# One add on 128 channels for a batch's logits, filling products ahead of the last slot products, and new places for every step of the plan

## The chip, the cores and the metric

The kernel runs on one core of a Trainium2 chip. The metric is the device time of one execution in microseconds (us). The engines go by the profile's names: PE is TensorE (PEld its weight loads), DVE VectorE, ACT ScalarE, POOL GpSimd, SP the engine whose queue issues most DMAs.

## The reference

Attention within hash buckets over 4 batches of 8 heads, 768 positions of 64 numbers each, then a soft mixture of 8 experts with 4 slots each over the 3072 x 512 result.

```python
q_bits = (np.einsum('bhsd,dk->bhsk', q, proj) > 0)      # six bits, a bucket number
mask = q_bucket[:, :, :, None] == k_bucket[:, :, None, :]
scores = np.where(mask, scale * (q @ k.T), -1e9)
attn = softmax(scores); x = attn @ v                     # per head
...
logits = x @ phi                                         # 3072 x 32
d = exp(logits - logits.max(0)); d /= d.sum(0) + 1e-09
slot_input = d.T @ x                                     # per expert: 4 slots of 512
h = maximum(slot_input[e] @ w1[e], 0); slot_out[e] = h @ w2[e]
c = exp(logits - logits.max(1)); c /= c.sum(1) + 1e-09
return c @ slot_out
```

## The kernel before, in words

All 32 heads run through one software pipeline, two heads (a pair) at a time. For a pair, `load` (482) brings q and k in two DMAs into the buffers raw0 and raw1, which have one copy each; `bits` (635) projects them; `split_hi` (581) casts both to a high half on ACT (592) and `split_lo` (594) takes the rest: for x = 0 on DVE (from head 4 on), for x = 1 on POOL, both at line 596 and both from two SBUF inputs. `spread_*` and `move` (598) bring these into the operands X and Y, by DMA on SP's queue. `first_x`, `first_y` and the like do the same for the first heads.

For a head h, `smax` (683) makes 12 products with the bits, into PSUM tiles of a pool with two buffers; `most` (697) takes row maxima of them on DVE and so gives the buffers back; `shift` and `shift_rows` (724, 737) turn the maxima into a row that one more DMA (mr) writes into X and Y. `scores(h, i, part)` (747) makes the scores with that row, into PSUM tiles of a pool with three buffers, `exps(h, n)` (758) exponentiates a tile on ACT and gives its buffer back. `acc(h, n)`, n = 1 to 5 (764), adds up exponentials on POOL, 128 x 768 at a time; the last head's n > 2 run on DVE. `av(h, i)` (774) multiplies with v. `acc(h, 2)` needs exponentials that `exps(h, 4)` and `exps(h, 6)` make, `acc(h, 4)` those of 8 and 10, `acc(h, 5)` those of 10 and 11.

For a pair, `pair_sum`, `pair_turn`, `pair_rec` (789 to 811) make the reciprocals of the row sums, `pair_log` and `pair_add` (813, 822) the share of the pair in its batch's logits, `pair_x` (839) the outputs. After four pairs the batch is done: `batch_both` (885) adds the two halves of the logits, `batch_max` (896) is a chain of small DVE instructions, `batch_exp`, `batch_turn`, `batch_slots` (949, 48 products into the slots, 957), `batch_weigh`, `batch_share`, `batch_arrange` do the rest. The last batch does this in a tail of its own (`one_*`, `batch_fold`, `batch_slots`), then the experts' two layers run (1190 on) on weights that `load_weights` (466) brings piece by piece.

The order is written out by hand: `at` (1043) gives every step a due place, from the table FIRST for the first heads, LAST for the last ones, else WHEN (its lists have one entry for even and one for odd heads), in units of a sixth of a head, and the plan is sorted by it (1128). Each engine and SP's queue take their instructions in the order of the sorted plan, and wait there for what they need.

Of the kernel before, what the change touches and what calls it, by code (L numbers as in the profile page):

```python
# [9 lines left out]
F32 = mybir.dt.float32  # L10
F32R = mybir.dt.float32r
AF = mybir.ActivationFunctionType
ALU = mybir.AluOpType
# [32 lines left out]
WHEN = {'load': -18.5437,  # L46
 'bits': -14.5981,
 'bits_over': -14.5078,
 'split_hi': -9.9694,
 'split_lo': [-9.8385, -9.8378],  # L50
 'spread': [[-9.8341, -9.7926, -8.3674, -3.7564], [-9.232, -8.9609, -8.9193, -8.8534]],
 'load_v': [-2.0731, 0.304],
 'smax': [[-6.5818, -6.2731, -4.3769, -3.4458, -4.5967, -3.7676, -3.5906, -3.9389, -2.661, -2.8254, -2.6599, -3.084], [-8.0753, -7.9227, -7.3452, -6.8708, -5.9483, -2.1659, -2.1447, -5.982, -2.2765, -1.3212, -1.255, -1.427]],
 'scores': [[4.5824, 6.3832, 6.4644, 4.2001, 3.9067, 7.1017, 7.7467, 5.1054, 8.1238, 5.4296, 7.4038, 5.2071], [2.8436, 2.465, 2.9648, 2.4657, 5.7327, 3.0748, 3.2444, 3.2884, 4.4451, 6.0219, 6.0296, 4.6638]],
 'shift': [-2.4326, -0.5749],
 'shift_rows': [-2.1527, 0.4391],
 'acc': [[8.5792, 9.0133, 10.0698, 10.5707, 12.1884], [4.5656, 6.6965, 8.4071, 9.7438, 9.7613]],
 'av': [[7.8325, 8.0552, 9.4787, 9.5207, 9.724, 9.7353], [6.5159, 6.7171, 8.6714, 9.1161, 9.1578, 9.6194]],
 'pair_sum': 21.4738,
 'pair_turn': 21.5156,  # L60
 'pair_rec': 21.5212,
 'pair_log': 21.5499,
 'pair_x': [25.7118, 30.2518],
 'pair_add': 22.5706,
 'batch_both': 24.1116,
 'batch_max': 26.5961,
 'batch_exp': 31.1234,
 'batch_turn': 32.6363,
 'batch_scale': 58.0306,
 'batch_slots': 33.1739,  # L70
 'batch_weigh': 32.9664,
 'batch_share': 33.3424,
 'batch_arrange': 33.3585,
 'load_weights': 29.1076,
 'most': [[-5.7734, -3.5266, -3.0352, -3.6373, -3.1083, -3.355, -2.5228, -2.4882, -2.8978], [-6.6907, -6.2627, -5.1645, -3.8385, -1.1223, -4.3733, -2.2387, -0.7783, -0.8368]],
 'exps': [[5.4955, 6.513, 5.4191, 5.1659, 8.0415, 5.6129, 8.4248, 8.0422, 5.629], [3.1683, 3.4874, 2.9413, 6.3976, 3.6406, 5.4799, 6.1309, 6.353, 8.0514]]}

FIRST = {('bits', 0): -102.0988,
 ('first_x', 0): -24.247,
 ('first_x', 1): -39.392,  # L80
 ('first_x', 2): -29.078,
 ('first_x', 3): -19.8151,
 ('load', 4, 0): -5.2093,
 ('load', 4, 1): -3.4609,
 ('bits', 2): -21.6367,
 ('split_hi', 2): -5.8363,
 ('split_lo', 2, 0): 0.2624,
 ('split_lo', 2, 1): -4.3782,
 ('spread_y', 2): -4.8648,
 ('spread_bits', 2): -12.8087,  # L90
 ('spread_l', 2): 6.144,
 ('spread_x', 2): 3.6219,
 ('smax', 1, 0, 0): -22.4884,
 ('smax', 1, 0, 1): -14.425,
 ('smax', 1, 1, 0): -13.675,
 ('smax', 1, 1, 1): -18.5454,
 ('smax', 1, 2, 0): -15.9696,
 ('smax', 1, 2, 1): -10.3836,
 ('smax', 1, 3, 0): -10.2744,
 ('smax', 1, 3, 1): -13.2403,  # L100
# [1242 lines left out]
```

## Time and profile before

| | |
|---|---|
| runs shown | 481.4, 485.52, 1116.75 us; median 485.52 us |
| the profiled execution | 484.55 us |
| its span, first to last instruction | 482.8 us |
| PE busy | 452.3 us, 94% |
| DVE, ACT, POOL busy | 361.5, 276.9, 356.2 us |
| mean granted TensorE clock | 0.972 |

The profile shows one execution. A row of a timeline has the start in us from the span's start, the duration in us, the engine (a q behind it: its sequencer, here an issued DMA), the line, the operation, out<-in, the shape, how many ran in a row, and in brackets how long the engine idled before and what ended the wait. A granted clock of 1.00 is TensorE's level of 2.4 GHz, 0.50 that of 1.2 GHz.

### The profile page before, as it was taken

Reading aid. Unit: us, or ns where it says so; the run is one execution under the profiler, and the core shown is the slowest. Engines: PE = TensorE matmul, PEld = TensorE weight load, DVE = VectorE, ACT = ScalarE, POOL = GpSimd, SP = SyncE. Lnnn points to the kernel's source line nnn. Section 1 sums busy time; section 2 is a strip of 40 time slices with the busy share of each in tenths; the row PEclk is TensorE's granted clock in tenths of the full one; section 3 lists DMA queues with packets and bytes.
Section 4 is the critical chain, followed back from the end, with each engine's and each line's share of the span. In section 5 each row is a group of like instructions: output and inputs, shape, how many; then the busy total and the mean of one; then the engine's idle time right before and its main releaser. Section 6 shows DMA issues by size and latency. Waiting matters only on the chain.

```text
span 482.8 us, 10644 instructions
## 1 busy us (share of the span) xinstructions
PE 452.3 (94%) x3975; PEld 280.5 (58%) x3975; DVE 361.5 (75%) x669; ACT 276.9 (57%) x568; POOL 356.2 (74%) x223
## 2 busy tenths in 40 slices
PE   8999999999959999999959999899789999979993
PEld 6756565656637574747545656565365665434572
DVE  5868787878797878797988878687978783574142
ACT  5747575757555666665735858475645755522231
POOL 8499798989893898979866999798938999710000
PEclk9999999999988999999979999999979999989998
DMA  6575556576637575857546665757365279998977
GB/s 190 123 190 159 136 150 152 164 160 210 153 92 205 135 216 150 226 139 228 136 142 143 202 157 169 201 170 176 98 183 128 67 167 331 342 380 331 412 302 304
DMA packets 37703, 93.18 MB, mean 193 GB/s; under 512 B 7106, under 2 KB 13380, under 8 KB 37652
## 3 DMA queue, kind: packets, MB, share of 16 engines
q1 hardware_dynamic: 37380, 92.11, 64.9%
q8 instruction: 31, 0.51, 0.4%
q10 hardware_dynamic: 240, 0.34, 0.2%
q14 instruction: 20, 0.16, 0.1%
q0 software_dynamic: 32, 0.07, 0.0%
HBM read 52.76 MB, written 6.29 MB: 122 GB/s over the span
## 4 chain that ended last, share of the span: by engine, by line
PE 85%; DVE 6%; DMA 4%; ACT 2%; issue 1%; SPq 0%; DVEq 0%; ACTq 0%
PE st L755 28%; PE av L782 23%; PE smx L692 15%; DVE w L596 4%; PE qs L1251 3%; PE qh L1198 3%; PE mi L639 3%; PE mi L794 2%; PE mi L819 2%; DMA w<-w 1%; PE mi L740 1%; PE av L548 1%; DMA XY<-mr 1%; PE mi L957 1%; ACT w L592 1%
## 5 line engine op out<-in xcount | busy, mean ns | idle before, releaser
L772 POOL TENSOR_TENSOR acc<-acc,pt 128x768 f32<-128x768 f32 x125 | 232.7, 1865 | 11.9 <-ACT pt L761 6.7
L761 ACT ACTIVATE pt<-st 128x512 f32<-128x512 f32 x288 | 163.5, 594 | 89.0 <-PE st L755 87.2
L755 PE MATMUL st<-XY 128*128 128x256 f32 (+1 forms) x768 | 181.4, 348 | 2.1 <-DMA XY<-mr 1.2
L704 DVE TENSOR_REDUCE mx<-smx 128x1 f32<-128x512 f32 x192 | 131.6, 688 | 49.0 <-PE smx L692 46.3
L755 PEld LDWEIGHTS st<-XY 128*128 128x128 f32 x768 | 127.7, 194 | 23.6 <-issue 4.5
L692 PE MATMUL smx<-XY 96*128 96x256 f32 (+1 forms) x384 | 123.2, 362 | 15.6 <-DVE mx L704 14.8
L782 PE MATMUL av<-pt,v 128*32 128x384 f32 x1536 | 137.7, 489 | 0.0
L692 PEld LDWEIGHTS smx<-XY 96*128 96x128 f32 x384 | 71.4, 194 | 49.0 <-DVE mx L704 18.8
L782 PEld LDWEIGHTS av<-pt,v 128*32 128x32 f32 x1536 | 45.4, 109 | 67.7 <-issue 55.0
L769 POOL TENSOR_TENSOR acc<-pt 128x768 f32<-128x768 f32 x32 | 58.6, 1832 | 32.9 <-ACT pt L761 32.9
L701 DVE TENSOR_REDUCE mx<-smx 128x2 f32<-128x512 f32 x96 | 65.6, 685 | 4.7 <-PE smx L692 3.8
L596 DVE TENSOR_TENSOR w<-raw,w 128x768 fp32r<-128x768 f32 x14 | 37.5, 2677 | 1.9 <-issue 0.5
L596 POOL TENSOR_TENSOR w<-raw,w 128x768 fp32r<-128x768 f32 x16 | 35.1, 2196 | 0.0
L797 ACT ACTIVATE sm<-mi,eps 128x384 f32<-128x384 f32 x15 | 8.7, 579 | 30.4 <-PE mi L794 30.4
L592 ACT CAST w<-raw 128x768 fp32r<-128x768 f32 x30 | 23.6, 831 | 0.5 <-DMA XY<-w 0.2
L609 ACT CAST XY<-w 64x768 fp32r<-64x768 f32 x30 | 23.3, 825 | 0.0
L786 ACT COPY avs<-av 128x384 f32<-128x384 f32 x32 | 15.2, 476 | 12.2 <-PE av L782 12.0
L842 DVE TENSOR_TENSOR xq<-mi,r 128x384 f32<-128x384 f32 x30 | 16.7, 558 | 2.2
L841 DVE STREAM_TRANSPOSE mi<-avs 128x384 f32<-128x384 f32 x30 | 17.4, 582 | 0.8 <-ACT mr L743 0.7
L811 ACT COPY r<-rt 64x12 f32<-64x12 f32 x60 | 11.9, 199 | 7.1 <-DVE rt L803 6.4
L1251 PE MATMUL qs<-w 128*32 128x128 f32 (+1 forms) x360 | 14.9, 304 | 0.0
L801 DVE STREAM_TRANSPOSE sm<-sm 128x384 f32<-128x384 f32 x15 | 8.7, 578 | 7.4 <-ACT sm L797 7.2
(174 smaller groups left out, 337.4 us busy)
## 6 DMA issues: line engine op xcount, KB each, us to landing
w<-w SPq DMA_DIRECT2D x61, 512.0 KB
XY<-w SPq DMA_DIRECT2D x47, 384.0 KB
XY<-w SPq DMA_DIRECT2D x63, 192.0 KB
raw<-qk SPq DMA_DIRECT2D x30, 384.0 KB
v<-vt SPq DMA_DIRECT2D x32, 192.0 KB
out<-w SPq DMA_DIRECT2D x9, 512.0 KB
xq<-w SPq DMA_DIRECT2D x3, 512.0 KB
out<-w SPq DMA_DIRECT2D x5, 256.0 KB
```

Source lines behind the costliest of these rows:

```text
L592: nc.scalar.copy(st[h]["w4"][:, 2 * x], st[h]["raw", x])
L596: (nc.vector if h > 2 and x == 0 else nc.gpsimd).tensor_tensor(out=w[:, 2 * x + 1], in0=st[h]["raw", x], in1=w[:, 2 * x], op=ALU.subtract)
L609: nc.scalar.copy(s["Y"][0:64, x], s["w4"][0:64, 2 * x])
L692: nc.tensor.matmul(pt[:, o:o + b - a], s["Y"][0:96, 0, t * P:(t + 1) * P], s["Y"][0:96, 1, a:b], start=True, stop=True)
L701: nc.vector.tensor_reduce(out=mx[:, n - 1:n + 1], in_=s["sm_ps", n - 1].rearrange("p (a x) -> p a x", a=2), axis=AX.X, op=ALU.max)
L704: nc.vector.reduce_max(out=mx[:, n:n + 1], in_=s["sm_ps", n], axis=AX.X)
L755: nc.tensor.matmul(pt[:, o:o + b - a], x[:, 1, i * P:(i + 1) * P], x[:, 0, a:b], start=first, stop=not first)
L761: nc.scalar.activation(s["P", n // 4][:, 512 * u:512 * u + 512], s["st_ps", n - (n % 4 == 2)], AF.Exp, scale=D ** -0.5)
L769: nc.gpsimd.tensor_tensor(out=s["acc"], in0=pr[:, 0:S], in1=pr[:, S:2 * S], op=ALU.add)
L772: eng.tensor_tensor(out=s["acc"], in0=s["acc"], in1=pr[:, a * S:(a + 1) * S], op=ALU.add)
L782: nc.tensor.matmul(s["av"][2 * e + 32 * c:2 * e + 32 * c + 32, 0:HC], s["v"][:, i, e:e + 32], pr[:, o + c * HC:o + (c + 1) * HC], start=(i ...
L1251: nc.tensor.matmul(pos[i][32 * j:32 * j + 32, 0:w], hTs[g][:, f, 32 * j:32 * j + 32], wt[1, x, 2 * g + f // 4, j][:, (f % 4) * HM + o:(f % ...
```

## The change

`batch_both` copies both halves of the logits crosswise on ACT (two copies of 64 x 384) and adds them in one POOL instruction on 128 channels; before it was one copy and two adds on 64 channels. `slots_of` takes the two PSUM tiles of the slots; for the last batch `slots_warm` takes them and issues three products of `ones` with `ident` into them, just ahead of `batch_fold` and `batch_slots`; their result is overwritten.

All values of WHEN, FIRST and LAST are replaced. Sorted, they give these orders around a batch's end (the first batch, heads 0 to 7, ends while heads 8 and 9 are in their scores and the low halves of heads 12 and 13 are made; without batch_both and batch_max it is the order of every pair):

| | before | after |
|---|---|---|
| POOL | acc(8,3), acc(9,1), acc(8,4), batch_both, acc(8,5), acc(9,2), split_lo(12,1), acc(9,3), acc(9,4), acc(9,5) | acc(8,3), acc(8,4), acc(9,1), acc(8,5), batch_both, acc(9,2), acc(9,3), split_lo(12,1), acc(9,4), acc(9,5) |
| ACT | pair_sum, exps(9,2), pair_rec, exps(9,6), av copy, mr copy, exps(9,7), batch_both, exps 9: 8, 10, 4, split_hi(12), exps(9,11) | pair_sum, exps 9: 2, 7, 6, av copy, mr copy, pair_rec, exps(9,8), batch_both, exps 9: 11, 4, 10, split_hi(12) |
| DVE | most 11: 0, 2, 3, 7, pair_x, most(11,4), split_lo(12,0), batch_max, most 11: 8, 6, 11, 10 | most 11: 0, 2, 3, 7, 4, pair_x, split_lo(12,0), batch_max, most 11: 8, 6, 11, 10 |
| PE, scores of head 9 ahead of av | 4 0, 5 1, 2 0, 4 1, 5 0 | 4 0, 5 1, 4 1, 5 0, 2 0 |
| SP | spread_bits, spread_l, load_weights, both loads, load_v, mr | spread_bits, load_weights, spread_l, load_v, both loads, mr |

In the tail, one_r and one_rec of head 30 come ahead of the last head's sums on DVE, and all av products of the last head ahead of one_sum(31). The diff, cut to the values of steps that are spoken of:

```diff
-WHEN = {'load': -18.5437,
+WHEN = {'load': -16.9234,
- 'split_hi': -9.9694,
+ 'split_hi': -11.2327,
- 'split_lo': [-9.8385, -9.8378],
+ 'split_lo': [-8.8537, -10.0635],
- 'load_v': [-2.0731, 0.304],
+ 'load_v': [-2.0194, 0.6857],
- 'scores': [[4.5824, 6.3832, 6.4644, 4.2001, 3.9067, 7.1017, 7.7467, 5.1054, 8.1238, 5.4296, 7.4038, 5.2071], [2.8436, 2.465, 2.9648, 2.4657, 5.7327, 3.0748, 3.2444, 3.2884, 4.4451, 6.0219, 6.0296, 4.6638]],
+ 'scores': [[5.5336, 6.5595, 7.2456, 5.3311, 4.8322, 7.6515, 7.8464, 5.8622, 8.3628, 7.2153, 7.2449, 6.0119], [2.9829, 3.2589, 3.3422, 2.8511, 5.6361, 2.9563, 3.2566, 3.4627, 4.4862, 5.1968, 5.5762, 4.7924]],
- 'acc': [[8.5792, 9.0133, 10.0698, 10.5707, 12.1884], [4.5656, 6.6965, 8.4071, 9.7438, 9.7613]],
+ 'acc': [[8.3761, 8.826, 9.5057, 10.2774, 11.0382], [5.0375, 6.238, 7.6971, 8.2168, 8.677]],
- 'pair_rec': 21.5212,
+ 'pair_rec': 22.3657,
- 'batch_both': 24.1116,
+ 'batch_both': 23.3631,
- 'batch_max': 26.5961,
+ 'batch_max': 27.5587,
- 'exps': [[5.4955, 6.513, 5.4191, 5.1659, 8.0415, 5.6129, 8.4248, 8.0422, 5.629], [3.1683, 3.4874, 2.9413, 6.3976, 3.6406, 5.4799, 6.1309, 6.353, 8.0514]]}
+ 'exps': [[6.8485, 7.9413, 5.9426, 5.2012, 8.5439, 6.9083, 9.1384, 8.8492, 7.1258], [3.3029, 3.7302, 3.1641, 6.1125, 3.8755, 3.858, 4.9531, 6.2821, 6.0829]]}
- 'load_weights': 29.1076,
+ 'load_weights': 33.735,
...
- ('one_r', -2): 1.4545,
+ ('one_r', -2): -2.3986,
- ('one_rec', -2): 3.1261,
+ ('one_rec', -2): -2.3733,
- ('acc', -1, 3): -0.0546,
+ ('acc', -1, 3): -0.8523,
- ('acc', -1, 5): 0.7717,
+ ('acc', -1, 5): 1.774,
- ('one_sum', -1): 0.8847,
+ ('one_sum', -1): 1.8742,
...
@@ -886,9 +886,9 @@
 
         lacc = lacc_of[b]
         dl = bst[b]["dl"] = dp.tile([P, HC], F32, name="dl", bufs=1)
-        nc.scalar.copy(dl[0:64], lacc[64:128])
-        for x in (1, 0):
-            nc.gpsimd.tensor_tensor(out=dl[64 * x:64 * x + 64], in0=lacc[0:64], in1=dl[0:64], op=ALU.add)
+        for x in range(2):
+            nc.scalar.copy(dl[64 * x:64 * x + 64], lacc[64 - 64 * x:128 - 64 * x])
+        nc.gpsimd.tensor_tensor(out=dl, in0=lacc, in1=dl, op=ALU.add)
 
     def logits_of(b):
         return bst[b]["lg"][:, 0:HC] if b == B - 1 else bst[b]["dl"]
@@ -946,10 +946,20 @@
         if b < B - 1:
             turn_logits(b, z["dl"])
 
+    def slots_of(b):
+        pool = p_st if b == B - 1 else p_mi
+        bst[b]["slots"] = [pool.tile([P, 512], F32, name=names[pool])[:, 0:DM // 2] for _ in range(2)]
+
+    def slots_warm(b, n):
+        slots_of(b)
+        for _ in range(n):
+            nc.tensor.matmul(bst[b]["slots"][0][0:32, 0:P], ones, ident, start=True, stop=True)
+
     def batch_slots(b):
         z = bst[b]
-        pool = p_st if b == B - 1 else p_mi
-        pts_x = [pool.tile([P, 512], F32, name=names[pool])[:, 0:DM // 2] for _ in range(2)]
+        if b < B - 1:
+            slots_of(b)
+        pts_x = z["slots"]
         for j in range(0, 2 * NT, 4):
             for x in range(2):
                 rows = slice(64 * x, 64 * x + 64)
@@ -1166,6 +1176,7 @@
         f(*args)
 
 
+    slots_warm(B - 1, 3)
     batch_fold()
     batch_slots(B - 1)
     spin_in(2, 1, p_av)
```

## Rows read from the trace of the kernel before

**Rows 1.** The page, part 1: busy us, share of the span, instructions.

```profile
PE 452.3 (94%) x3975; PEld 280.5 (58%) x3975; DVE 361.5 (75%) x669; ACT 276.9 (57%) x568; POOL 356.2 (74%) x223
```

**Rows 2.** Busy time by stretch; columns us, PE, PEld, DVE, ACT, POOL, clock, DMA.

```profile
102.27:125.79 23.52, 23.52 (x198) 14.85 (x202) 19.40 (x36) 15.61 (x31) 20.49 (x12) 1.00 0.68 186
125.79:158.11 32.32, 27.43 (x246) 17.23 (x250) 28.34 (x50) 16.75 (x35) 22.18 (x14) 0.89 0.50 137
228.77:260.92 32.15, 27.20 (x246) 16.93 (x250) 28.35 (x49) 16.94 (x36) 22.09 (x14) 0.89 0.51 138
333.02:365.83 32.81, 27.86 (x246) 17.64 (x250) 28.46 (x49) 16.96 (x36) 22.14 (x14) 0.90 0.50 136
```

**Rows 3.** Groups by line, the slot products: busy us, mean ns | idle before.

```profile
L957 PE MATMUL mi<-xq,avs 64*32 64x256 f32 x144 | 4.6, 380 | 0.0
L957 PE MATMUL st<-xq,avs 64*32 64x256 f32 x48 | 2.8, 624 | 1.4 <-DVE avs L944 1.4
```

**Rows 4.** Timeline of PE in the first batch pair: start, us, [idle <-releaser].

```profile
144.22 0.80 PE L692 MATMUL smx<-XY 96*128 96x512 f32 x1 [4.89 <-DVE mx L704]
```

**Rows 5.** Timeline of DVE, the same stretch.

```profile
135.62 6.60 DVE L596 TENSOR_TENSOR w<-raw,w 128x768 fp32r<-128x768 f32 x1
142.15 0.54 DVE L902 TENSOR_REDUCE ml<-dl 64x1 f32<-64x384 f32 x1
143.48 0.68 DVE L704 TENSOR_REDUCE mx<-smx 128x1 f32<-128x512 f32 x1
```

**Rows 6.** VectorE's instructions of line 596: duration ns min/median/max.

```profile
L596 DVE TENSOR_TENSOR w<-raw,w x14: 972/1784/6612, 41.1 to 375.6; 128x768 fp32r<-128x768 f32 x14
```

**Rows 7.** Timeline of POOL, the same stretch.

```profile
132.17 2.10 POOL L891 TENSOR_TENSOR dl<-lacc,dl 64x384 f32<-64x384 f32 x2
134.23 3.61 POOL L772 TENSOR_TENSOR acc<-acc,pt 128x768 f32<-128x768 f32 x2
137.80 1.85 POOL L596 TENSOR_TENSOR w<-raw,w 128x768 fp32r<-128x768 f32 x1
139.60 6.17 POOL L772 TENSOR_TENSOR acc<-acc,pt 128x768 f32<-128x768 f32 x3
```

**Rows 8.** Timeline of POOL in three narrow windows.

```profile
59.43 1.84 POOL L772 TENSOR_TENSOR acc<-acc,pt 128x768 f32<-128x768 f32 x1
...
61.35 1.83 POOL L772 TENSOR_TENSOR acc<-acc,pt 128x768 f32<-128x768 f32 x1
...
141.48 4.29 POOL L772 TENSOR_TENSOR acc<-acc,pt 128x768 f32<-128x768 f32 x2
```

**Rows 9.** Timelines of an ordinary pair by engine; the last row ACT at the border.

```profile
63.83 1.56 ACT L592 CAST w<-raw 128x768 fp32r<-128x768 f32 x2
...
64.75 1.79 DVE L596 TENSOR_TENSOR w<-raw,w 128x768 fp32r<-128x768 f32 x1
...
63.88 1.85 POOL L772 TENSOR_TENSOR acc<-acc,pt 128x768 f32<-128x768 f32 x1 [0.70 <-ACT pt L761]
65.69 2.56 POOL L596 TENSOR_TENSOR w<-raw,w 128x768 fp32r<-128x768 f32 x1
...
68.36 0.40 PE L692 MATMUL smx<-XY 96*128 96x512 f32 x1
...
133.59 1.09 ACT L761 ACTIVATE pt<-st 128x512 f32<-128x512 f32 x2 [1.08 <-PE st L755]
```

**Rows 10.** Groups by line, the batch's adds and copies.

```profile
L891 POOL TENSOR_TENSOR dl<-lacc,dl 64x384 f32<-64x384 f32 x6 | 6.1, 1009 | 0.5
L992 POOL TENSOR_TENSOR lacc<-sm,cm 128x192 f32<-128x192 f32 x3 | 1.5, 508 | 9.7 <-DVE cm L991 9.7
L889 ACT COPY dl<-lacc 64x384 f32<-64x384 f32 x3 | 1.5, 493 | 0.0
```

**Rows 11.** Timeline of SP's queue in the ordinary pair.

```profile
71.65 0.81 SPq L600 DMA_DIRECT2D XY<-mr  x1
```

**Rows 12.** Busy time by stretch, the tail's slot products; columns as in rows 2.

```profile
432.00:435.40 3.40, 3.40 (x52) 1.95 (x52) 1.42 (x7) 0.57 (x2) 0.00 (x0) 0.50 0.94 347
```

More of the change, by code (lines that the diff above doesn't have):

```diff
@@ new lines @@
+WHEN = {'load': -16.9234,
+ 'bits': -14.3717,
+ 'bits_over': -14.2655,
+ 'split_hi': -11.2327,
+ 'split_lo': [-8.8537, -10.0635],
+ 'spread': [[-10.9434, -8.8759, -5.5323, -4.0719], [-9.1735, -8.8228, -9.2009, -8.7942]],
+ 'load_v': [-2.0194, 0.6857],
+ 'smax': [[-5.575, -5.3023, -4.4327, -3.0295, -4.0086, -3.6335, -3.5262, -3.6649, -2.6064, -2.4574, -2.4398, -2.9107], [-7.944, -7.6273, -7.2504, -7.1653, -6.0491, -1.7544, -1.1252, -6.235, -2.2797, -0.308, -0.306, -0.5541]],
+ 'scores': [[5.5336, 6.5595, 7.2456, 5.3311, 4.8322, 7.6515, 7.8464, 5.8622, 8.3628, 7.2153, 7.2449, 6.0119], [2.9829, 3.2589, 3.3422, 2.8511, 5.6361, 2.9563, 3.2566, 3.4627, 4.4862, 5.1968, 5.5762, 4.7924]],
+ 'shift': [-2.3114, 0.6368],
+ 'shift_rows': [-2.0369, 1.2347],
+ 'acc': [[8.3761, 8.826, 9.5057, 10.2774, 11.0382], [5.0375, 6.238, 7.6971, 8.2168, 8.677]],
+ 'av': [[8.2731, 8.3246, 9.7304, 9.8775, 9.8827, 9.9536], [6.3913, 6.4111, 8.4627, 8.834, 8.8375, 9.6647]],
+ 'pair_sum': 21.6006,
+ 'pair_turn': 21.816,
+ 'pair_rec': 22.3657,
+ 'pair_log': 21.8834,
+ 'pair_x': [26.9559, 31.3802],
+ 'pair_add': 22.6172,
+ 'batch_both': 23.3631,
+ 'batch_max': 27.5587,
+ 'batch_exp': 32.2161,
+ 'batch_turn': 32.4089,
+ 'batch_scale': 38.5308,
+ 'batch_slots': 33.428,
+ 'batch_weigh': 33.4073,
+ 'batch_share': 33.5326,
+ 'batch_arrange': 33.6799,
+ 'load_weights': 33.735,
+ 'most': [[-5.349, -4.1424, -2.8414, -3.7102, -3.3152, -3.3833, -2.3128, -2.33, -2.6082], [-6.0949, -4.6558, -4.0, -3.3235, -0.4133, -3.3242, -1.3496, 0.6306, -0.0306]],
+ 'exps': [[6.8485, 7.9413, 5.9426, 5.2012, 8.5439, 6.9083, 9.1384, 8.8492, 7.1258], [3.3029, 3.7302, 3.1641, 6.1125, 3.8755, 3.858, 4.9531, 6.2821, 6.0829]]}
```

644 lines of the change are left out of this document (312 added, 332 removed).

## The prediction

> **What bounds the kernel now.** I read the page's busy shares first. TensorE is busy 94% of the span, so time can only come from where it is not [rows 1]. Next I cut the span at the first product of each pair's bit projection (line 639) and asked for busy time by stretch. An ordinary pair takes 23.52 us with TensorE busy in all of it; the three pairs in which a batch ends take 32.32, 32.15 and 32.81 us, TensorE idle for 4.9 us in each, at a mean granted clock of 0.89 to 0.90 [rows 2]. Batch work explains little: its 48 slot products are 4.6 us over three batches, 1.53 us each [rows 3]. An undisturbed batch pair would take 23.52 + 1.53 = 25.05 us; the three spend 7.27 + 7.10 + 7.76 = 22.13 us more.
>
> Then the timeline of one of them. TensorE waits 4.89 us, from 139.33, for a row maximum on VectorE, which gives back a PSUM buffer [rows 4]. VectorE is late through one instruction: the low half `split_lo(12,0)`, issued at 135.62, lasts 6.60 us; then batch_max's chain takes 143.48 - 142.15 = 1.33 us before the maximum [rows 5]. Alone that instruction takes 0.97 us, at the median 1.78 us [rows 6]. Beside it GpSimd runs with no gap from 134.23: `acc(8,5)`, `acc(9,2)`, `split_lo(12,1)`, `acc(9,3)` [rows 7]. `acc(9,4)`, the same head's next sum, starts at 141.48, after a gap of 0.08 us, and only there VectorE gets through [rows 7, 8]. Two sums of one head in a row leave such a gap elsewhere too (59.43 + 1.84 = 61.27, next start 61.35) [rows 8]. I read it so: both engines want the same way into SBUF; a train of GpSimd instructions each ready before the last ends keeps it, and VectorE enters where the train breaks. In an ordinary pair GpSimd has idled 0.70 us before `acc(h,2)` at 63.88, its next instruction is not ready yet, and VectorE, asking at 64.75, waits 0.8 us [rows 9].
>
> The trace shows the lock. The Trainium skill (SBUF — State Buffer, "Who interferes with whom") says that a VectorE instruction with two SBUF inputs and a GpSimd one that reads SBUF exclude each other, and that whichever issues first has the port for its whole instruction. By that VectorE would have followed the instruction running at its issue, at about 136.0, and there would be no 5 us to recover: the sum would be the old time less the shorter add, which is the second rival below. The trace differs, three more GpSimd instructions went ahead, and it decides.
>
> **The change part by part.**
> *One add on 128 channels.* GpSimd loses two instructions on 64 channels of 1.01 us each with the gap between them (2.10 us in the timeline) and gets one of 128 x 384 [rows 7, 10]. The trace has none of this shape: 128 x 192 takes 0.51 us, so 1.02 us by columns; 128 x 768 takes 1.84 us, an upper end [rows 8, 10]. I take 1.02, as both nearer rows agree. ScalarE makes two copies for one, +0.49 us [rows 10]. Three times each.
>
> *GpSimd's order around the batch.* Sums now run `acc(8,3)`, `acc(8,4)`, `acc(9,1)`, `acc(8,5)`, batch_both, `acc(9,2)`, `acc(9,3)`, `split_lo(12,1)`, `acc(9,4)`, `acc(9,5)`. `acc(8,4)` uses input ready long before, where GpSimd now waits for an exponential. With the shorter batch_both, GpSimd has no backlog at `acc(9,2)`. And `acc(9,3)` directly follows `acc(9,2)`: a break in the train lies where VectorE asks.
>
> ScalarE decides when. At the border it now does pair_rec's reciprocal copies and the second copy of the logits ahead of the exponentials, but need not wait the 1.08 us for scores that it waits there now; `exps(9,4)` ended at 133.59 + 1.09 = 134.68 [rows 9], and I keep 134.6. Another exponential (half of 1.09) and the first cast (half of 1.56) follow [rows 9], so VectorE asks near 135.9. `acc(9,2)` runs from 134.6 to 136.4. VectorE enters there, ends at 137.3; batch_max to 138.65, the maximum (0.68) to 139.3. TensorE wants the buffer at 139.33 [rows 4]: a stall of 0 to 0.2 us for 4.9, too short for the clock to fall. At the 1.84 us end for the add everything is 0.8 us later, 2.4 us over three batches.
>
> *The same order in the eleven ordinary pairs with such a low half on VectorE.* There VectorE asks while `acc(h,2)` runs and the break follows; it waits under 1.84 us, as today. The GpSimd half comes one sum later (+1.84 us), less an earlier start of up to 0.7 us, as the scores for `exps(h,4)` move behind fewer products. It ends at 69.4 to 70.1 in that pair, now 65.69 + 2.56 = 68.25 [rows 9]. Behind it on SP's queue stand the second raw load, then the move of mr, issued at 71.65 [rows 11]: a margin of 1.5 to 2.2 us, so I cost it at nothing. load_weights goes in front of that stretch, load_v in front of the loads; both wait for nothing late. If the margin went, the following head's scores would wait by the excess.
>
> *TensorE's order.* The same products; single scores and maxima swap places. Ordinary pairs have no idle TensorE time to win. I take 0, with 0.1 us a pair either way, 1.5 us in all.
>
> *Start and tail.* The first 40 us keep their work in another order; I take 0, 2 us either way. In the tail VectorE makes head 30's reciprocals before the last sums, worth up to 1.3 us if that chain ends last, and DMA is nearly full there: I take 0. The three filling products wait for no late result and lie in TensorE's 1.4 us wait ahead of the slot products [rows 3]: cost 0, or at most three short products if that cover goes. Now those 48 products run at 624 ns at a granted clock of 0.50 (the 1.2 GHz level), against 380 ns for the same shape in mid-kernel [rows 3, 12]; at the higher level they would take 1.3 us less. I take 0, since three products after several sparse microseconds are little.
> The Trainium skill (TensorE: Matmul & The Clock Gate, "HAM oscillation — how this bites in real kernels") says that TensorE falls to the lower level in idle gaps and must be kept active. The trace agrees as to the fall after each border stall (0.89). By the rule the fillings help, -1.3 us; no run here shows that three suffice.
>
> **Sum.** The profiled execution took 484.55 us (span 482.8), 0.2% under the 485.52 us median; another run took 481.4. 484.55 - 22.13 + 3 x 0.1 = 462.7 us.
>
> **Rivals.**
> *One place late.* VectorE misses the break, or batch_max and the low half together leave it behind: a stall of 1.84 us in each batch pair, and the clock's share (7.27 - 4.89 = 2.4 us) with it. 462.7 + 3 x 4.24 = 475.4. For: VectorE had 28.3 us of work and waiting in these pairs [rows 2], and my border timeline has 0 to 0.2 us to spare. Against: it idles 23.52 - 19.40 = 4.1 us in an ordinary pair [rows 2].
> *The lock stays.* The train still holds at the borders, or the port is not what releases VectorE: 484.55 less at most three times the 1.08 us of GpSimd work, 481 to 484. For: `acc(9,2)`, `acc(9,3)`, `split_lo(12,1)`, `acc(9,4)` are still four in a row. Against: the hand-over at 141.48 came just between sums of one head.
> *Slower: the train starves every pair.* Place: the gap between `acc(h,2)` and `acc(h,3)`. If it is no entry, VectorE gets in only between `acc(h,4)` and `acc(h,5)`, four instructions of 1.8 us after an `acc(h,2)` at 63.1: 70.3, plus 0.97 and 0.69 makes 72.0, where TensorE wants its buffer at 68.36 [rows 9]. That is 3.6 us in each of eleven pairs that are full today, with the borders as they are: 484.55 + 39.6 = 524, and 551 if the clock falls each time (2.4 us more). It decides by whether one 0.08 us gap is enough. For: the one that was enough is seen only at the three borders, with VectorE waiting long. Against: there it sufficed three times in three.
>
> **How the numbers follow.** Forecast, stalls gone (457 to 469): 0.65. One place late (469 to 476): 0.14. The lock stays, or another small loss eats the gain (476 to 494): 0.15. Slower: 0.06. A measurement of this kernel tells about 2%, 9.7 us, from no change. Faster by more than that is the first case and nearly all of the second, 0.79; within it 0.15; slower 0.06. The range goes down by the start's 2 us, the tail and clock (2.6) and the pairs (1.5), to 457; up to the end of the second case, 476.
>
> **What would show it.** In the profile after: three batch pairs near 25 us; no row of VectorE's low half over 2.5 us; no TensorE wait of several us on line 692's buffer; granted clock 1.00 through the attention; one batch_both add near 1.0 us. Wrong, if ordinary pairs exceed 23.8 us, if a 6 us low half remains, or if mr's move arrives after TensorE asks. Slot products near 380 ns at the end would show the fillings at work.

## The result and the profile after

The changed kernel takes 466.64 us (median of four runs, 466.26 to 467.38), 0.965 of the time before, with a 95% interval of 0.960 to 0.971; one run of the kernel before that took 1116.75 us is left out of this ratio. The profiled execution took 467.38 us, its span 465.6 us. The forecast was 462.7 us. The page's first part, TensorE:

```profile
PE 449.5 (97%) x3981; PEld 276.1 (59%) x3981; DVE 341.7 (73%) x669; ACT 277.8 (60%) x571; POOL 352.6 (76%) x220
```

TensorE is busy 97% of the span instead of 94% [rows 1]. Busy time by stretch, cut as in [rows 2] at the first product of a pair's bit projection (columns as there): an ordinary pair, the first and the last of the three pairs in which a batch ends, and all that comes behind.

```profile
102.32:125.83 23.51, 23.51 (x202) 14.71 (x198) 18.87 (x37) 15.60 (x31) 20.50 (x12) 1.00 0.69 185
125.83:151.36 25.53, 25.53 (x250) 15.54 (x246) 22.59 (x51) 17.18 (x36) 21.89 (x13) 1.00 0.64 176
318.99:344.59 25.60, 25.59 (x250) 15.53 (x246) 22.61 (x50) 17.31 (x37) 21.89 (x13) 1.00 0.65 176
344.59:465.60 121.01, 107.27 (x1144) 60.80 (x1136) 65.40 (x133) 50.95 (x118) 51.48 (x39) 0.95 0.77 274
```

The three batch pairs take 25.53, 25.61 and 25.60 us, where they took 32.15 to 32.81 [rows 2]; TensorE is busy throughout, at the full clock. The last stretch, the tail, is the surprise. The kernel before needed less for it:

```profile
365.83:482.80 116.97, 105.03 (x1142) 59.54 (x1142) 62.79 (x134) 50.89 (x118) 53.36 (x40) 0.97 0.80 281
```

Up to 78.49 us, where the fifth pair starts, both traces run level; from there to the end of the third batch pair the kernel saved 365.83 - 344.59 = 21.24 us; the tail cost 121.01 - 116.97 = 4.04 us in these two executions.

The first border of the changed kernel, timelines of VectorE and then of GpSimd:

```profile
135.34 1.36 DVE L596 TENSOR_TENSOR w<-raw,w 128x768 fp32r<-128x768 f32 x1
137.96 0.68 DVE L704 TENSOR_REDUCE mx<-smx 128x1 f32<-128x512 f32 x1
...
132.87 1.00 POOL L891 TENSOR_TENSOR dl<-lacc,dl 128x384 f32<-128x384 f32 x1 [1.80 <-ACT dl L890]
134.04 4.36 POOL L772 TENSOR_TENSOR acc<-acc,pt 128x768 f32<-128x768 f32 x2 [0.17 <-ACT pt L761]
```

All its low halves on VectorE (ns: shortest, median, longest):

```profile
L596 DVE TENSOR_TENSOR w<-raw,w x14: 948/950/1404, 41.6 to 354.3; 128x768 fp32r<-128x768 f32 x14
```

And the group of the new add (busy us, mean ns, idle before):

```profile
L891 POOL TENSOR_TENSOR dl<-lacc,dl 128x384 f32<-128x384 f32 x3 | 3.0, 1005 | 5.4 <-ACT dl L890 5.4
```

VectorE asks for the low half at 135.34, while `acc(9,2)` runs (134.04 to 135.89). It is through at 136.70, so it entered as that sum ended, and the first 0.6 us of `acc(9,3)` are the wait for it (the two rows of GpSimd together last 4.36 us instead of some 3.7). The maximum that gives TensorE its buffer starts at 137.96 instead of 143.48 [rows 5]. No low half lasts over 1.40 us, where three lasted 6.6 us [rows 6]. The one add takes 1005 ns, as estimated.

Now the tail: first the kernel before, TensorE's timeline at two of its waits:

```profile
427.37 1.57 PE L875 MATMUL smx<-avs,phs 128*64 128x384 f32 x8 [0.49 <-DVE avs L865]
431.91 2.80 PE L957 MATMUL st<-xq,avs 64*32 64x256 f32 x48 [1.38 <-DVE avs L944]
```

The kernel before, the last add of EPS (`one_r`, line 858; ns):

```profile
L858 DVE TENSOR_SCALAR rt<-dl x1: 173/173/173, 425.8 to 425.8; 128x12 f32<-128x12 f32 x1
```

The changed kernel, timelines of TensorE, VectorE and GpSimd:

```profile
404.33 0.85 PE L850 MATMUL st<-acc,ones 128*32 128x384 f32 x8 [1.54 <-DVE acc L772]
409.19 1.54 PE L875 MATMUL smx<-avs,phs 128*64 128x384 f32 x4 [3.21 <-DVE avs L865]
413.42 1.49 PE L956 MATMUL st<-ident,ones 128*32 128x128 f32 x6
414.84 2.81 PE L967 MATMUL st<-xq,avs 64*32 64x256 f32 x48
...
397.53 1.60 DVE L858 TENSOR_SCALAR rt<-sm 128x12 f32<-128x12 f32 x1
405.86 1.73 DVE L858 TENSOR_SCALAR rt<-dl 128x12 f32<-128x12 f32 x1
...
397.27 1.83 POOL L772 TENSOR_TENSOR acc<-acc,pt 128x768 f32<-128x768 f32 x1
405.82 0.76 POOL L1168 DMA_DIRECT2D fold<-cst  x1 [6.72 <-DVE dl L856]
406.58 0.98 POOL L1171 MEMSET siT<- 128x1024 f32 x1
```

In the kernel before each add of EPS (the 1e-09 of the reference) to the 128 x 12 sums takes 0.17 us. In the changed one the first takes 1.60 us, beside GpSimd's last sum (397.27 to 399.10), and the second 1.73 us, beside the issue of fold's transfer and siT's memset (405.82 to 407.56). Both end when GpSimd does. Counted from the start of the tail, the last logits of line 875 come 3.06 us later than before (64.60 against 61.54), and the slot products 4.17 us later (70.25 against 66.08). TensorE's wait of 3.21 us is followed by a long stretch at the lower level, 1.2 GHz (busy time by stretch, columns as in [rows 2]):

```profile
408.09:418.33 10.24, 9.14 (x74) 5.68 (x74) 5.39 (x19) 3.00 (x8) 0.00 (x0) 0.50 0.51 189
```

That is 10.24 us at a granted clock of 0.50, where the kernel before had 3.4 us [rows 12]. The three filling products lie inside it: 1.49 us (two rows of the trace each). The slot products' input is there at 414.03; they start at 414.84, when the filling is done.

### The profile page after: what moved, and what is told of

Read it like the earlier page. It is cut to its first block, busy times and chain, and to the rows that moved or that the text cites. A ratio compares the mean times of both kernels' runs of the same rounds, so it can differ in the third digit from the quotient of the medians.

```text
span 465.6 us, 10655 instructions
## 1 busy us (share of the span) xinstructions
PE 449.5 (97%) x3981; PEld 276.1 (59%) x3981; DVE 341.7 (73%) x669; ACT 277.8 (60%) x571; POOL 352.6 (76%) x220
## 4 chain that ended last, share of the span: by engine, by line
PE 88%; DVE 5%; DMA 2%; SPq 1%; ACT 1%; issue 1%; DVEq 0%; ACTq 0%
PE st L755 27%; PE av L782 25%; PE smx L692 16%; PE qs L1262 3%; PE qh L1209 3%; PE mi L639 2%; PE mi L794 2%; PE mi L819 2%; DMA XY<-mr 1%; PE mi L740 1%; PE av L548 1%; PE mi L967 1%; SPq L600 1%; PE qh L1285 1%; DMA raw<-qk 1%
## 5 line engine op out<-in xcount | busy, mean ns | idle before, releaser
L772 POOL TENSOR_TENSOR acc<-acc,pt 128x768 f32<-128x768 f32 x125 | 238.2, 1908 | 22.2 <-ACT pt L761 16.8
L761 ACT ACTIVATE pt<-st 128x512 f32<-128x512 f32 x288 | 160.1, 597 | 59.9 <-PE st L755 54.4
L755 PE MATMUL st<-XY 128*128 128x512 f32 (+1 forms) x768 | 174.4, 342 | 1.1 <-DMA XY<-mr 1.0
L755 PEld LDWEIGHTS st<-XY 128*128 128x128 f32 x768 | 122.0, 189 | 21.0 <-ACT pt L761 4.1
L692 PE MATMUL smx<-XY 96*128 96x256 f32 (+1 forms) x384 | 120.8, 356 | 0.7 <-DVE XY L632 0.3
L692 PEld LDWEIGHTS smx<-XY 96*128 96x128 f32 x384 | 69.6, 190 | 34.0 <-DVE mx L704 14.2
L596 POOL TENSOR_TENSOR w<-raw,w 128x768 fp32r<-128x768 f32 x16 | 29.4, 1842 | 1.8 <-ACT w L592 1.8
L592 ACT CAST w<-raw 128x768 fp32r<-128x768 f32 x30 | 23.5, 833 | 2.1 <-DMA XY<-w 1.8
L609 ACT CAST XY<-w 64x768 fp32r<-64x768 f32 x30 | 23.5, 831 | 0.0
L596 DVE TENSOR_TENSOR w<-raw,w 128x768 fp32r<-128x768 f32 x14 | 14.7, 1047 | 1.1 <-ACT w L592 1.1
L1209 PE MATMUL qh<-w,siT 128*32 128x512 f32 x128 | 14.1, 594 | 0.0
L639 PE MATMUL mi<-raw,pb 128*32 128x384 f32 x120 | 13.4, 491 | 0.5 <-DMA raw<-qk 0.5
```

Source lines behind the costliest of these rows:

```text
L592: nc.scalar.copy(st[h]["w4"][:, 2 * x], st[h]["raw", x])
L596: (nc.vector if h > 2 and x == 0 else nc.gpsimd).tensor_tensor(out=w[:, 2 * x + 1], in0=st[h]["raw", x], in1=w[:, 2 * x], op=ALU.subtract)
L692: nc.tensor.matmul(pt[:, o:o + b - a], s["Y"][0:96, 0, t * P:(t + 1) * P], s["Y"][0:96, 1, a:b], start=True, stop=True)
L755: nc.tensor.matmul(pt[:, o:o + b - a], x[:, 1, i * P:(i + 1) * P], x[:, 0, a:b], start=first, stop=not first)
L761: nc.scalar.activation(s["P", n // 4][:, 512 * u:512 * u + 512], s["st_ps", n - (n % 4 == 2)], AF.Exp, scale=D ** -0.5)
L772: eng.tensor_tensor(out=s["acc"], in0=s["acc"], in1=pr[:, a * S:(a + 1) * S], op=ALU.add)
```

## The experiments

Two questions. At the borders: is it the one add, or the new order, that lets VectorE in, and by what rule? In the tail: is it the two adds of EPS, the clock, or the filling? Five runs are for the first, seven for the second; `acc(9,2)` and the like name the first border's steps, the other two borders behave alike.

One thing must be known before the runs of the tail are read: the length of the stretch at the lower clock differs from run to run with the same instructions. The runs "two adds on 64 channels" and "half moved back" (both below) change nothing in the tail. Busy time of the tail and TensorE at line 875, first for the two adds, then for the half moved back:

```profile
346.23:463.90 117.67, 104.45 (x1144) 59.88 (x1136) 65.39 (x133) 50.70 (x118) 51.53 (x39) 0.97 0.79 282
409.87 0.87 PE L875 MATMUL smx<-avs,phs 128*64 128x384 f32 x4 [3.21 <-DVE avs L865]
...
345.17:465.20 120.03, 106.11 (x1144) 60.80 (x1136) 65.40 (x133) 50.95 (x118) 51.55 (x39) 0.95 0.77 276
```

Both have the same long adds of EPS (1.60 to 1.61 and 1.73 us) and the same wait of some 3.2 us as the changed kernel's profile. But the stretch at 0.50 lasts 3.41 us in the first and 6.83 us in the second, against 10.24 us, and the tail 117.67 and 120.03 us, against 121.01. So a shorter stretch in one trace of an edited tail does not show that the edit shortened it.

### The one add alone

In the kernel before:

```
-        nc.scalar.copy(dl[0:64], lacc[64:128])
-        for x in (1, 0):
-            nc.gpsimd.tensor_tensor(out=dl[64 * x:64 * x + 64], in0=lacc[0:64], in1=dl[0:64], op=ALU.add)
+        for x in range(2):
+            nc.scalar.copy(dl[64 * x:64 * x + 64], lacc[64 - 64 * x:128 - 64 * x])
+        nc.gpsimd.tensor_tensor(out=dl, in0=lacc, in1=dl, op=ALU.add)
```

> The kernel before with one edit: batch_both adds on 128 channels in one instruction; order of all steps as before. Theory (VectorE enters the port only where GpSimd's train breaks, and a sum directly behind a sum of the same head is the break): acc(9,2), split_lo(12,1), acc(9,3) still run ahead of the break at acc(9,4), only up to 1.1 us sooner, so the low half on VectorE still takes some 5.5 us at each border and the time falls by 3 x 1.1 us at most, to 481-484 us. Rival (the shorter add takes the backlog away and that alone lets VectorE in): low half under 2.5 us, no stall, 462-468 us.

Measured: 465.0 us (463.53 to 469.43), 0.959 of before (0.954 to 0.964). My theory fell. Timelines of VectorE and GpSimd in this run:

```profile
136.03 2.08 DVE L596 TENSOR_TENSOR w<-raw,w 128x768 fp32r<-128x768 f32 x1 [0.44 <-issue]
...
133.66 3.62 POOL L772 TENSOR_TENSOR acc<-acc,pt 128x768 f32<-128x768 f32 x2
137.25 2.55 POOL L596 TENSOR_TENSOR w<-raw,w 128x768 fp32r<-128x768 f32 x1
```

And busy time in two stretches of it, the first batch pair and the tail (columns as in [rows 2]):

```profile
125.86:152.10 26.24, 25.84 (x246) 15.52 (x250) 23.73 (x50) 17.16 (x36) 21.35 (x13) 1.00 0.63 170
347.29:462.30 115.01, 103.31 (x1142) 59.19 (x1142) 62.78 (x134) 50.91 (x118) 53.46 (x40) 0.99 0.81 285
```

GpSimd runs as I had expected, without a gap: `acc(8,5)`, `acc(9,2)`, `split_lo(12,1)`. But VectorE gets in all the same, between `acc(9,2)` and `split_lo(12,1)`: its low half takes 2.08 us, and the GpSimd half 2.55 instead of 1.85. No break between two sums of one head was needed. The batch pair takes 26.24 us, 0.7 us more than in the changed kernel; the tail, in the old order, takes 115.01 us at a clock of 0.99, 6.0 us less than in the changed one.

### The new order alone, in two ways

The kernel before, with GpSimd's half behind `acc(h-3,3)`:

```
- 'split_lo': [-9.8385, -9.8378],
+ 'split_lo': [-9.8385, -9.55],
```

> The kernel before with one number changed: GpSimd's split_lo(h,1) goes behind acc(h-3,3) instead of ahead of it, so two sums of one head lie next to each other where VectorE asks; batch_both stays two adds. Theory (a break between two sums of one head is the entry): the break is at the end of acc(9,2), 137.85 us instead of 141.4 us, the low half takes some 3.2 us instead of 6.6, the TensorE stall falls from 4.9 us to about 1.5 us, and the clock may hold: 467-475 us. Rival (the order of the half does not matter, the backlog of batch_both does): low half stays at 6.6 us, 484 us.

Measured: 469.15 us (466.83 to 471.0), 0.966 (0.962 to 0.970). Timelines of VectorE, GpSimd and TensorE in this run:

```profile
135.93 3.02 DVE L596 TENSOR_TENSOR w<-raw,w 128x768 fp32r<-128x768 f32 x1
...
134.52 6.11 POOL L772 TENSOR_TENSOR acc<-acc,pt 128x768 f32<-128x768 f32 x3
...
140.94 0.50 PE L692 MATMUL smx<-XY 96*128 96x512 f32 x1 [1.30 <-DVE mx L704]
```

As the theory said: the row of GpSimd holds `acc(8,5)`, `acc(9,2)` and `acc(9,3)`. VectorE is kept out at the end of the first (136.34) and let in at the end of the second (138.13), the break between two sums of one head; the low half takes 3.02 us, TensorE waits 1.30 us, and the clock does not fall.

The changed kernel with batch_both as before, two adds on 64 channels (the diff above, turned round):

> The changed kernel with batch_both as before: one copy and two adds on 64 channels; order and filling products as changed. Theory (order decides): GpSimd is about 1.1 us later at acc(9,2), VectorE enters at its end near 136.9 us, low half some 2.5 us, a TensorE stall of 0 to 1.1 us at each border: 467-470 us. Rival (the one add decides): low half 6 us or more again, stalls of 4.9 us, 480-488 us.

Measured: 466.13 us (465.47 to 466.94), 0.960 (0.957 to 0.963), as good as the change itself. The order alone suffices, as the theory said, but its delay did not come: VectorE asks at 134.85, its low half takes 1.83 us instead of 2.5, and the time is just below the theory's range. Timelines of VectorE and TensorE in this run:

```profile
134.85 1.83 DVE L596 TENSOR_TENSOR w<-raw,w 128x768 fp32r<-128x768 f32 x1
...
138.67 0.50 PE L692 MATMUL smx<-XY 96*128 96x512 f32 x1 [0.41 <-DVE mx L704]
```

So either part does it. With the old order the one add is enough; with the new order the one add is not needed.

### The changed kernel with the half moved back

```
- 'split_lo': [-8.8537, -10.0635],
+ 'split_lo': [-8.8537, -10.35],
```

> The changed kernel with one number changed: GpSimd's split_lo(h,1) goes back ahead of acc(h-3,3), which takes the two sums apart. Theory (the break between two sums of one head is the entry): acc(9,2), split_lo(12,1), acc(9,3) run as one train, VectorE enters near 139.6 us instead of 135.8, low half 4 us or more, a TensorE stall of some 3 us at each border with the clock's fall behind it: 475-484 us. Rival (any hand-over will do as long as GpSimd had idled before the instruction that runs when VectorE asks; acc(9,2) starts there after 0.17 us of idle time): low half 1.4 us at the borders, 1.8 us in ordinary pairs, 465-468 us.

Measured: 466.67 us (465.98 to 467.0), 0.961 (0.958 to 0.963). The rival wins. Timelines of VectorE and GpSimd in this run:

```profile
135.90 1.41 DVE L596 TENSOR_TENSOR w<-raw,w 128x768 fp32r<-128x768 f32 x1
...
134.65 1.84 POOL L772 TENSOR_TENSOR acc<-acc,pt 128x768 f32<-128x768 f32 x1 [0.16 <-ACT pt L761]
136.52 2.49 POOL L596 TENSOR_TENSOR w<-raw,w 128x768 fp32r<-128x768 f32 x1
```

`acc(9,3)` no longer follows `acc(9,2)`, but `split_lo(12,1)` became ready only as `acc(9,2)` ended, and VectorE went first. The entry is not a place in the program; it is a hand-over, here one for which GpSimd's next instruction had only just become ready. In ordinary pairs the low half mostly does not wait (median 0.95 us), where the rival had 1.8.

### A copy added to the kernel before

From these runs I had a rule in numbers, how long before a hand-over the next GpSimd instruction was ready, and put it to the test by making ScalarE slower:

```
+    pad_t = pp.tile([P, P], F32, name="pad_t")
...
+    def pad_copy(b):
+        nc.scalar.copy(pad_t, ident)
...
+            at(p0 + 24.38, pad_copy, h // H)
```

> The kernel before with work added: one small ScalarE copy (128 x 128, some 0.25 us) directly ahead of exps(9,4) at each of the three borders; nothing taken away, GpSimd's order and adds as before. New theory (from the hand-overs of the runs so far: VectorE gets in between two GpSimd instructions that follow each other without a gap if the second became ready 1.25 us or less before the end of the first, and is kept out at 1.35 us or more): acc(9,2) becomes ready 0.25 us later, 1.1 us instead of 1.39 us before the end of acc(8,5), VectorE enters there, near 136.0 us, low half 1-1.5 us instead of 6.6, no stall: 461-468 us. Rival (only a gap in the train or less GpSimd work lets VectorE in): the train is as gapless and as long as before, low half 6 us or more, 483-487 us.

Measured: 484.9 us (482.1 to 487.9), 1.002 (0.999 to 1.006): no change. The rule with its threshold of 1.25 us fell. Timelines of VectorE and GpSimd (lines are one higher here):

```profile
136.65 6.40 DVE L597 TENSOR_TENSOR w<-raw,w 128x768 fp32r<-128x768 f32 x1 [0.32 <-issue]
...
135.03 3.63 POOL L773 TENSOR_TENSOR acc<-acc,pt 128x768 f32<-128x768 f32 x2
138.63 1.84 POOL L597 TENSOR_TENSOR w<-raw,w 128x768 fp32r<-128x768 f32 x1
140.44 6.16 POOL L773 TENSOR_TENSOR acc<-acc,pt 128x768 f32<-128x768 f32 x3
```

The copy did its part: it took 0.30 us, and `acc(9,2)` became ready 1.03 us before the end of `acc(8,5)`. VectorE was still kept out at three hand-overs, and its low half took 6.40 us. What is left after all fourteen traces is a count. I took every hand-over between two GpSimd instructions at which a low half on VectorE was waiting (from 50 us on; one low half can wait through several), and for each the end of the ScalarE instruction that makes the next one's input. Where GpSimd had a gap (0.03 us or more), before the running instruction or behind it, VectorE went in every time: 113 hand-overs, 76 of them with more than 0.2 us between its request and the hand-over. Where there was a gap on neither side, it went in 4 times, all with the next instruction ready 0.63 us or less before the hand-over, and was kept out 21 times, all with the next one ready 1.02 us or more before it. These 25 are few places: 3 of the 4 are one hand-over of the run with the one add at its three borders, and the 21 are seven, of three kernels, at three borders each. Which of the two engines was ready first does not decide: `split_lo(12,1)` became ready 0.64 us after VectorE had asked both in the run with the one add, where VectorE went in ahead of it, and in this run, where it did not. What decides between 0.63 and 1.02 us, and by which mechanism, stays open.

### The tail: no filling products

```
-    slots_warm(B - 1, 3)
+    slots_warm(B - 1, 0)
```

> The changed kernel with no filling products (0 instead of 3). Theory (the three products start only when the products ahead of them on TensorE are done, run at the lower clock and end 0.9 us after the slot products' input is there, so they are pure cost): the slot products start some 0.8 us sooner, clock as before, 465.5-466 us. Rival (they hold the clock): the low stretch gets longer and the time rises to 467-468 us.

Measured: 468.4 us (466.18 to 469.39), 0.969 (0.964 to 0.974); inconclusive. The slot products start 67.9 us after the start of the tail instead of 70.25, but the stretch at the lower clock, 10.24 us again, starts 2.4 us later in the tail and reaches into the first layer's products, and the span is 465.9 us, as with the filling. Neither theory gets its time; the interval overlaps that of the change.

### The tail: the memset on VectorE

```
-            nc.gpsimd.memset(siT, 0.0)
+            nc.vector.memset(siT, 0.0)
```

> The changed kernel with siT's memset in the tail moved from GpSimd to VectorE, into the 0.97 us in which VectorE idles before one_r of the last head. Theory (that add of EPS took 1.73 us instead of 0.17 because GpSimd's DMA issue and memset held the port beside it): the add falls to 0.9 us if the DMA issue holds the port too, to 0.17 if not; TensorE's wait of 3.21 us falls to 1.7-2.3 us, and the stretch at the lower clock gets shorter: 462-465.5 us. Rival (the add is slow for another reason): add still 1.7 us, time 466-467.5 us.

Measured: 466.17 us (464.7 to 466.87), 0.964 (0.960 to 0.968). The add of EPS is back at 0.17 us, so it was GpSimd that held it. Timelines of VectorE and TensorE:

```profile
405.16 0.91 DVE L1171 MEMSET siT<- 128x1024 f32 x1 [1.22 <-PE st L850]
406.55 0.17 DVE L858 TENSOR_SCALAR rt<-dl 128x12 f32<-128x12 f32 x1
...
408.31 1.18 PE L875 MATMUL smx<-avs,phs 128*64 128x384 f32 x4 [2.67 <-DVE avs L865]
```

But the memset did not fit into VectorE's idle time. It took 0.91 us from 405.16 and put the transposition off to 405.99, so TensorE's wait fell only from 3.21 to 2.67 us; the lower clock lasted 6.83 us, as it also does with the half moved back. The time is above the theory's range. Whether the issue of the transfer alone holds the port can't be read here: it ended before the add began.

### The tail: the adds of EPS on ScalarE

```
-        nc.vector.tensor_scalar_add(r, tt.rearrange("p (j x) -> p j x", x=32)[:, :, 0], EPS)
+        nc.scalar.activation(r, tt.rearrange("p (j x) -> p j x", x=32)[:, :, 0], AF.Identity, bias=eps)
```

> The changed kernel with the two adds of EPS in one_r on ScalarE instead of VectorE. Theory (VectorE's tensor_scalar waits for GpSimd's instructions: 1.60 and 1.73 us instead of 0.17): the reciprocals behind them, 0.23 us, don't wait; two hand-overs of some 0.3 us come in; 3.0 - 0.7 = 2.3 us less on the chain, and less time at the lower clock: 461-464.5 us. Rival (any VectorE instruction there waits for GpSimd): the reciprocals take 1.6 us and the time stays at 466-467 us.

Measured: 463.36 us (462.11 to 465.84), 0.959 (0.955 to 0.964). Theory confirmed as to the adds, and the time lies in its range. Timelines of ScalarE (the two adds) and TensorE (the two waits):

```profile
397.33 0.31 ACT L858 ACTIVATE rt<-sm,eps 128x12 f32<-128x12 f32 x1 [1.81 <-DVE sm L856]
405.51 0.31 ACT L858 ACTIVATE rt<-dl,eps 128x12 f32<-128x12 f32 x1 [2.04 <-DVE dl L856]
...
403.97 0.85 PE L850 MATMUL st<-acc,ones 128*32 128x384 f32 x8 [0.25 <-DVE acc L772]
407.34 0.87 PE L875 MATMUL smx<-avs,phs 128*64 128x384 f32 x4 [1.72 <-DVE avs L865]
```

The adds take 0.31 us each, the waits fall from 1.54 to 0.25 us and from 3.21 to 1.72 us, and the reciprocals stay at 0.23 us. The lower clock lasts 6.83 us instead of 10.24, which alone shows nothing, since it does so too with the half moved back; at that same length the tail is 118.28 us here and 120.03 there.

### The tail: filling in the wait itself

```
+    at(last + 6, slots_warm, B - 1, 12)
...
-    slots_warm(B - 1, 3)
```

> The changed kernel with 12 filling products in place of 3, and these moved into TensorE's wait of 3.21 us ahead of the last head's logits instead of directly ahead of the slot products. Theory (that wait is what lets the clock fall for 10.24 us): the clock stays at 1.00 there, the slot products take 380 ns instead of 631 ns and the turned weights' products get shorter too: 462-464.5 us. Rival (so little work does not hold the clock): same low stretch, only the 0.9 us of the three late products is saved: 465.5-466 us.

Measured: 465.3 us (463.14 to 468.15), 0.963 (0.958 to 0.968). TensorE's timeline:

```profile
405.07 2.81 PE L956 MATMUL st<-ident,ones 128*32 128x128 f32 x24
408.36 0.87 PE L875 MATMUL smx<-avs,phs 128*64 128x384 f32 x4 [0.48 <-DVE avs L865]
412.14 2.65 PE L967 MATMUL st<-xq,avs 64*32 64x256 f32 x48 [1.31 <-DVE avs L944]
```

Not shown either way. Twelve products (24 rows, 2.81 us) leave 0.48 us of the wait, and the clock stays at 1.00 through the products behind it, 0.87 us for line 875 where the change had 1.54. But the runs with no filling products and with two adds on 64 channels leave the wait of 3.21 us open and have 0.87 us there too, so the filling need not be the cause. Behind the next wait, 1.31 us ahead of the slot products, the clock falls for 3.41 us, as long as with the two adds: most of these products run at the lower level (2.65 us for 48).

### The tail: order, and combinations

The changed kernel with the old order of the tail's reciprocals:

```
- ('one_r', -2): -2.3986,
- ('one_rec', -2): -2.3733,
- ('one_mul', -2): 0.6174,
+ ('one_r', -2): 1.9,
+ ('one_rec', -2): 3.1261,
+ ('one_mul', -2): 4.0867,
...
- ('one_r', -1): 9.2041,
- ('one_rec', -1): 9.7292,
- ('one_mul', -1): 9.7695,
+ ('one_r', -1): 3.3517,
+ ('one_rec', -1): 3.5221,
+ ('one_mul', -1): 5.1082,
```

> The changed kernel with six numbers of LAST changed, so that in the tail VectorE adds the last sums first and then does both heads' reciprocals together, as in the kernel before; three filling products kept. Theory (of the 4.0 us by which the tail grew, most comes from the two adds of EPS that now meet GpSimd's last sum and its memset): both adds take 0.17 us, the last head's logits start some 2.8 us sooner, and with the shorter wait the stretch at the lower clock goes from 10.24 us to 3.4 us or none: 460-464 us. Rival (the tail is set by DMA and by the weights' loads): 465.5-467 us.

Measured: 465.07 us (464.0 to 466.67), 0.962 (0.958 to 0.966). Timelines of VectorE, GpSimd and TensorE:

```profile
403.01 1.74 DVE L858 TENSOR_SCALAR rt<-dl 128x12 f32<-128x12 f32 x1
...
402.98 0.76 POOL L1168 DMA_DIRECT2D fold<-cst  x1 [5.13 <-DMA w<-w]
403.74 0.98 POOL L1171 MEMSET siT<- 128x1024 f32 x1
...
406.12 2.83 PE L875 MATMUL smx<-avs,phs 128*64 128x384 f32 x8 [3.79 <-DVE avs L865]
```

The first add is free of GpSimd (0.18 us). The second is not: the issue of fold's transfer and the memset, which wait for a weight's transfer, come forward too, to 402.98, and meet the add again (1.74 us). TensorE waits 3.79 us, and the lower clock lasts 10.24 us, as in the changed kernel. The time lies between the theory's range and the rival's.

The same without the filling products:

> The kernel of the run with the old tail order and, in addition, no filling products. Theory (in that order TensorE waits some 1.4 us ahead of the slot products, the three products lie in it, cost nothing and hold no clock): within 0.8 us of the run with them. Rival (they hold the clock there): 1.3 us slower than with them. Second rival (they end after the slot products' input is there): 0.4-0.9 us faster.

Measured: 466.08 us (463.55 to 467.57), 0.963 (0.958 to 0.968): the two can't be told apart. The lower clock lasts 13.65 us. TensorE waits only 0.60 us ahead of the slot products there, so the cover that the expectation speaks of was not in this kernel either.

ScalarE's adds and 8 filling products in the wait:

> The changed kernel with both edits that helped the tail alone: the adds of EPS on ScalarE, and filling products (8, for a shorter wait) in TensorE's wait ahead of the last head's logits. Theory (they work on different terms, the lock and the clock): 460.5-463.5 us. Rival (the wait of 1.7 us that is left with the adds on ScalarE is too short for the filling to change anything): the same as with the adds alone, 463-464 us.

Measured: 464.0 us (462.46 to 465.04), 0.959 (0.955 to 0.963): no better than the adds alone, as the rival had it, though not for its reason. The wait ahead of line 875 is gone, but the clock falls later, for 6.83 us behind the next wait, as TensorE's timeline shows:

```profile
410.82 2.30 PE L967 MATMUL st<-xq,avs 64*32 64x256 f32 x48 [1.38 <-DVE avs L944]
```

The lowest medians are those of ScalarE's adds (463.36), of this last one (464.0) and of the one add alone (465.0). Their intervals all overlap that of the change (0.960 to 0.971), so that they are faster than it is not shown.

## Why the prediction was right, and where it was not

**The bound and its cause: right.** The forecast took three border stalls for the only large loss: 22.13 us, and 0.3 us left over. The stretch from 78.49 us to the last border gave 21.24 of it: the batch pairs 97.28 - 76.74 = 20.54 us, the pairs between them the other 0.7 us. Each batch pair is some 0.4 us longer than the 25.15 us of the sum.

**The border, step by step: right for this kernel.** `acc(9,2)` starts at 134.04, as its last exponential is done (134.6 was kept), VectorE asks at 135.34 (135.9), enters as `acc(9,2)` ends, and TensorE doesn't wait (0 to 0.2). One place late, the lock stays and the starved train did not happen; ordinary pairs stay at 23.5 to 23.83 us, with one of 24.09. Two are thus over the 23.8 us that the prediction named as a sign of being wrong; TensorE has no wait of 0.1 us or more from 60 us to the last border, so it is not mr's late move, and the kernel before had one of 24.97. In the ordinary pairs the low half on VectorE, which the prediction left waiting as today, mostly no longer waits (median 0.95 us instead of 1.78).

**Why VectorE enters: too narrow.** The prediction read the entry as the break between two sums of one head, and made the order the carrier of the gain, with the add as help. The runs show that the kernel before kept VectorE out only where a train with no gap met inputs that had been ready for 1.0 us or more. Alone, the one add brings GpSimd forward by 0.6 us and its second copy puts ScalarE back by 0.4 us; `split_lo(12,1)` is then ready only 0.6 us ahead of the hand-over instead of 1.6, and VectorE gets in. That either part alone removes the wait is shown; that the later readiness is what let VectorE in is read from the count, as the one run that only delayed an input (1.39 to 1.03 us ahead) changed nothing. They are two ways to one gain, and don't add up. The forecast came out right because it counted the stalls once.

At the border itself the page that the prediction weighed (the Trainium skill, SBUF — State Buffer, "Who interferes with whom": whichever issues first has the port for its instruction) stays at odds with the traces: in the run with the added copy VectorE asked at 136.65, and three GpSimd instructions that began later went ahead.

**Tail and filling products, "I take 0": mis-sized.** This is the step that failed: it measured +4.04 us in the profiled execution. With the 0.6 us by which the attention fell short, 462.7 + 4.0 + 0.6 = 467.3 us is the profiled execution's 467.38. The prediction saw the reciprocals of head 30 move ahead of the last sums and counted a gain of up to 1.3 us; it did not ask what GpSimd does beside the small add of EPS there. Moved, that add meets GpSimd's last sum, and the other one the memset: 1.43 and 1.56 us. The same section of the Trainium skill names `tensor_scalar` among the VectorE operations that can enter a two-port mode and then contend with GpSimd; this trace agrees as to the contention (0.17 us alone, 1.60 and 1.73 beside GpSimd; the mode itself it does not show), and the runs with the memset or the adds on another engine confirm it. The filling products' cover, TensorE's 1.4 us wait ahead of the slot products, had shrunk too, since TensorE's longest wait had moved ahead of line 875: without the filling 0.96 us of it were left, at the lower clock the filling takes 1.49 us, and its products end 0.8 us after the slot products' input was there. And they did not raise the clock here: the slot products take 631 ns, as before 624 [rows 3].

How much of the 4.04 us is the clock can be read only roughly. With the same tail, but 3.41 us at 0.50 as in the kernel before, the run with two adds on 64 channels has its last logits 2.10 us later than the kernel before (here 3.06), its slot products 1.84 us later (here 4.17) and its whole tail only 0.70 us longer. So beyond 0.7 us the loss came and went between executions of the same instructions, together with the length of that stretch; that the stretch made all of it is not shown, since 0.96 us of the difference is there when line 875 starts. The old tail itself took 115.0 to 115.8 us in the three runs that kept it and had no fall around the slot products. What sets the length of the stretch, 3.41 to 10.24 us behind the same wait, stays open.

## What to carry to other kernels

Where a VectorE instruction with two SBUF operands, or a small `tensor_scalar`, is many times longer than its twin elsewhere, look at what GpSimd does beside it, then at whether GpSimd's next instruction is ready early: a gap behind or before the running instruction, another order or a shorter instruction on GpSimd let VectorE in here; an input that was merely 0.36 us later did not. Before crediting a change with several edits, run each alone, since two of them may buy the same stall. And an instruction that is moved must be priced beside what it will then run next to, however small it was where it stood. What the clock costs in one trace should be held against a second trace of the same instructions before an edit is credited with it.

## What the runs showed of the hardware that was not expected

- A gapless train of GpSimd instructions let VectorE in where the next one had become ready 0.63 us or less before the hand-over (4 of 4, two places), and kept it out where it had been ready for 1.02 us or more (21 of 21, seven places at three borders each); with a gap on either side it was always let in (113 of 113).
- An add on 128 x 12 elements with one SBUF input waits for GpSimd as a 128 x 768 subtraction does, also for a transfer's issue followed by a memset: 1.73 us instead of 0.17.
- A wait of the same length does not always cost the clock, nor for as long. Behind the same 3.21 us wait the same tail had 3.41, 6.83 and 10.24 us at 0.50. The old order of the tail waits 1.38 us ahead of the slot products in the kernel before and in the run with the one add alone; the first had 3.4 us at 0.50 behind it, and the 48 products took 2.80 us; in the second the tail up to them ran at 1.00, and they took 1.53 us.
